# Per-head state products, a state decayed on GpSimd, and other places for a chunk's steps, in linear attention followed by an MLP

## The chip, the cores and the metric

One core of a Trainium2 chip. The metric is device time in microseconds (us) of one execution, the median of several runs. The core has TensorE (PE, matrix products; PEld is its weight load), VectorE (DVE), ScalarE (ACT), GpSimd (POOL) and SyncE (SP). They run side by side, each with its own instruction queue, and are tied together by semaphores. GpSimd and SyncE also issue the DMAs here.

## The reference

```python
# q, k, v: [4, 8, 768, 64] f32, lam: [8]; blocks of 64 positions, per head h
intra = (qb @ kb.T) * Dmask            # Dmask[i, j] = lam**(i - j) for i >= j, else 0
out   = intra @ vb + (qb * lam**(pos + 1)) @ kv_state
kv_state = lam**block * kv_state + (kb * lam**(block - 1 - pos)).T @ vb
# x: the heads' outputs side by side, [3072, 512]
h = x @ w_in                           # w_in [512, 2048]
g = 0.5 * h * (1 + erf(h / sqrt(2)))   # exact GELU
return g @ w_out                       # w_out [2048, 512], result [3072, 512] f32
```

The attention is a recurrence along the sequence: the 64 x 64 state of each head and batch is decayed and added to. The result feeds a two-layer MLP.

## The kernel before

**Chunks and groups.** The kernel works on chunks of C = 128 positions with all 8 heads: 24 chunks, numbered n, 6 per batch (`c.sb` is the place within the batch; the state starts anew at `sb` 0, and `sb` 5 needs no next state). Four chunks (M = 4) make a group of 512 rows for the MLP, so there are 6 groups. Matrix operands are bf16; the loads cast from f32 while they run, and are issued by GpSimd (L65 for q, k and v; L87 and L91 for slices of the two weights).

**A chunk's steps.** `begin` takes the loaded tiles, and `decay_k` makes k_dec (k times a decay) on GpSimd, or on ScalarE for chunks 0 and 1. k^T and q^T are made by TensorE in `transposes` (L178) for chunks 0 to 7, and by DMA in `dma_transposes` (L191 to L193) from chunk 8 on; q_hat is made on GpSimd there. `scores` (L200) multiplies k^T and q^T by pairs of heads into PSUM, and VectorE writes the masked result sc_m (L204). `next_state` forms the state for the next chunk. `outputs` adds, in PSUM, the product of state and q^T and the product of v and sc_m (L262), and the result goes to x_t, the MLP's input (L266 on ScalarE for the first four chunks, L268 on VectorE after).

**The state.** For chunks 0 to 2, `next_state` makes k_dec^T v per head (L215, eight matmuls of 64 columns), one VectorE add gives the new state (L227), and ScalarE makes a decayed copy, old (L230). The state's product in `outputs` is eight matmuls on 64 x 64 quarters of the array (L258). From chunk 4 on, the state is block-diagonal, two heads in each 128 x 128 block: `next_state_full` makes the product in four full matmuls (L237), VectorE adds the former state (tmp, L244) and multiplies by lam_blk, which holds the decay on the diagonal blocks and 0 elsewhere (L245), and `outputs` uses four full matmuls (L252). Chunk 3 crosses over: its state is written into first_blk, of which only the diagonal blocks are filled (L220).

**Order.** The schedule is manual: on each engine the instructions run in the order in which the program emits them. The opening, L341 to L386, is written out by hand: chunks 0 to 3, with idle matmuls (`keep_warm`, L350) between them. In the program, GpSimd's part is: the loads of chunks 0 to 3, w_in slice 0, k_dec of chunks 2 and 3, and then w_in slices 1 to 3, w_out slices 0 to 3 and (L418) the loads of chunks 4 to 7.

After it the MLP runs, group after group, in 32 blocks each: 16 of `mm1` (L280, four matmuls of 512 columns, then GELU on ScalarE, L282) and 16 quarters of `mm2` (L292; L307 in the last group). The attention of the next group's chunks is laid between these blocks: `todo` holds a step's kind (0 begin, 1 transposes, 2 scores and next state, 3 outputs) and its due time as a fraction of a group, and ahead of each block all steps that are due are emitted. The begin step also issues the loads of chunk n + 4 (`prefetch`). In groups from 1 on, the scores of the chunk with place i are due at 0.04 + 0.25 i, its outputs at 0.25 later (0.965 for the last), so the outputs of one chunk and the scores of the next are emitted together.

Of the kernel before, what the change touches and what calls it, by code (L numbers as in the profile page):

```python
# [8 lines left out]
F32 = mybir.dt.float32  # L9
BF16 = mybir.dt.bfloat16  # L10
ALU = mybir.AluOpType
ACT = mybir.ActivationFunctionType
# [3 lines left out]
def kernel(  # L16
# [10 lines left out]
    nc = tc.nc  # L27

    B, H, S, D = q.shape
    d_model, d_ff = moe_w_in.shape  # L30
    C = 128
    NB = S // C
    NCH = B * NB
    HP = H // 2
# [4 lines left out]

    M = 4  # L40
    NG = NCH // M
    assert NG * M == NCH and M < NB

    ctx.enter_context(tc.manual_schedule())

    consts = ctx.enter_context(tc.tile_pool(name="consts", bufs=1))
    w_pool = ctx.enter_context(tc.tile_pool(name="w", bufs=1))
    qkv_pool = ctx.enter_context(tc.tile_pool(name="qkv", bufs=8))
    work_pool = ctx.enter_context(tc.tile_pool(name="work", bufs=3))
# [52 lines left out]
    nc.vector.tensor_scalar(negj, pos, -1.0, None, op0=ALU.mult)  # L102
    nc.vector.tensor_scalar(cmj, pos, -1.0, float(C), op0=ALU.mult, op1=ALU.add)

    lam_blk = consts.tile([128, HP, 128], F32)
    first_blk = consts.tile([128, HP, 128], BF16)
    nc.vector.memset(lam_blk, 0.0)
    nc.vector.memset(first_blk, 0.0)


    ln = consts.tile([128, H], F32)
    ln_col = consts.tile([128, HP], F32)
# [2 lines left out]
    lam_m = consts.tile([128, H], F32)  # L115
    lam_k = consts.tile([128, H], F32)
    lam_c = consts.tile([128, HP], F32)
# [3 lines left out]
    for hi in range(2):  # L121
        p = slice(hi * D, (hi + 1) * D)
# [5 lines left out]
    nc.scalar.activation(lam_c, ln_col, ACT.Exp, scale=float(C))  # L128
    nc.scalar.activation(lam_p, ln, ACT.Exp, scale=pos)
    lam_c_b = lam_c[:, :, None].to_broadcast((128, HP, D))  # L130

    def make_lam_blk():
        for hi in range(2):
            p = slice(hi * D, (hi + 1) * D)
            nc.vector.tensor_copy(lam_blk[p, :, p], lam_c_b[p])

    def make_dmask():
        nc.vector.tensor_mul(dmask, cmask[:, None, :].to_broadcast((128, H, C)),
# [7 lines left out]
    states = {}  # L146

    def bank(shape, dtype, tag, name):
        return ps.tile(shape, dtype, tag=tag, name=name, bufs=2 if tag in ("sc", "mh", "mo") else 1)

    def begin(n, early=False):
        c = Chunk()
        c.n, c.sb, c.early = n, n % NB, early
        c.q, c.k, c.v = (raw.pop((n, name)) for name in "qkv")
        return c

    def decay_k(c, eng):

        if c.sb == NB - 1:
            return  # L160
        c.k_dec = work_pool.tile([128, H, D], BF16, tag="kd", name="k_dec")
        if eng is nc.scalar:
            for h in range(H):
                nc.scalar.activation(c.k_dec[:, h, :], c.k[:, h, :], ACT.Copy, scale=lam_k[:, h:h + 1])
        else:
            scale = lam_k if c.early else lam_m
            eng.tensor_mul(c.k_dec, c.k, scale[:, :, None].to_broadcast((128, H, D)))  # L167

    def transposes(c):
        if c.early:  # L170

            t_ps = [bank([128, HP, C], BF16, tag, "t_ps") for tag in ("mh", "mo")]
        else:
            both = bank([128, 2, HP, C], BF16, "t", "t_ps")
            t_ps = [both[:, 0], both[:, 1]]
        for dst, src in zip(t_ps, (c.k, c.q)):
            for hp in range(HP):
                nc.tensor.transpose(dst[:, hp, :], src[:, 2 * hp:2 * hp + 2, :], ident)  # L178
        c.kT = work_pool.tile([128, HP, C], BF16, tag="kT", name="kT")
        c.qT = work_pool.tile([128, HP, C], BF16, tag="qT", name="qT")  # L180
        if c.early and c.n % 2:
            nc.scalar.copy(c.kT, t_ps[0])
        else:
            nc.vector.tensor_copy(c.kT, t_ps[0])  # L184
        nc.vector.tensor_mul(c.qT, t_ps[1], lam_q)  # L185

    def dma_transposes(c):
        c.kT = work_pool.tile([128, HP, C], BF16, tag="kT", name="kT")
        c.qT = work_pool.tile([128, HP, C], BF16, tag="qT", name="qT")
        q_hat = work_pool.tile([128, H, D], BF16, tag="qh", name="q_hat")  # L190
        nc.sync.dma_start_transpose(out=c.kT, in_=c.k.rearrange("p h d -> p (h d)"))  # L191
        nc.gpsimd.tensor_mul(q_hat, c.q, lam_p[:, :, None].to_broadcast((128, H, D)))  # L192
        nc.sync.dma_start_transpose(out=c.qT, in_=q_hat.rearrange("p h d -> p (h d)"))  # L193
# [12 lines left out]
    def next_state(c):  # L206
        if c.sb == NB - 1:
            return
        if not c.early:
            return next_state_full(c)  # L210
        kv_ps = bank([128, HP, D], F32, "t", "kv_ps")
        for hp in range(HP):
            for hi in range(2):
                h = 2 * hp + hi
                nc.tensor.matmul(kv_ps[hi * D:(hi + 1) * D, hp, :], c.k_dec[:, h, :], c.v[:, h, :],  # L215
                                 start=True, stop=True)
        if c.n == M - 1:
            for hi in range(2):
                p = slice(hi * D, (hi + 1) * D)
                nc.vector.tensor_add(first_blk[p, :, p], kv_ps[p], states[c.n][1][p])  # L220
            states[c.n + 1] = first_blk, None
            return
        new = work_pool.tile([128, HP, D], BF16, tag="state", name="state")
        if c.sb == 0:
            nc.vector.tensor_copy(new, kv_ps)
        else:
            nc.vector.tensor_add(new, kv_ps, states[c.n][1])  # L227
        old = work_pool.tile([128, HP, D], F32, tag="old", name="old")
        for hp in range(HP):
            nc.scalar.activation(old[:, hp, :], new[:, hp, :], ACT.Copy, scale=lam_c[:, hp:hp + 1])  # L230
        states[c.n + 1] = new, old

    def next_state_full(c):

        kv_ps = bank([128, HP, 128], F32, "t", "kv_ps")
        for hp in range(HP):
            nc.tensor.matmul(kv_ps[:, hp, :], c.k_dec[:, 2 * hp:2 * hp + 2, :], c.v[:, 2 * hp:2 * hp + 2, :],  # L237
                             start=True, stop=True)
        new = work_pool.tile([128, HP, 128], BF16, tag="state_f", name="state")
        if c.sb == 0:  # L240
            nc.vector.tensor_mul(new, kv_ps, lam_blk)
        else:
            tmp = work_pool.tile([128, HP, 128], F32, tag="tmp", name="tmp")
            nc.vector.tensor_add(tmp, kv_ps, states[c.n][0])  # L244
            nc.vector.tensor_mul(new, tmp, lam_blk)  # L245
        states[c.n + 1] = new, None

    def outputs(c, x_t, off):
        o_ps = bank([128, HP, C], F32, "o", "o_ps")
        if c.sb > 0 and not c.early:  # L250
            for hp in range(HP):
                nc.tensor.matmul(o_ps[:, hp, :], states[c.n][0][:, hp, :], c.qT[:, hp, :],  # L252
                                 start=(hp == 0), stop=False, skip_group_check=True)
        elif c.sb > 0:
            for hp in range(HP):
                for hi in range(2):
                    p = slice(hi * D, (hi + 1) * D)
                    nc.tensor.matmul(o_ps[p, hp, :], states[c.n][0][p, hp, :], c.qT[p, hp, :],  # L258
                                     start=(hp == 0), stop=False, skip_group_check=True)
        for hp in range(HP):  # L260
            for hi in range(2):
                nc.tensor.matmul(o_ps[hi * D:(hi + 1) * D, hp, :], c.v[:, 2 * hp + hi, :], c.sc_m[:, hp, hi, :],  # L262
                                 start=(c.sb == 0 and hp == 0), stop=True, skip_group_check=True)
        x_o = x_t[:, :, off * C:(off + 1) * C]
        if c.early:
            nc.scalar.copy(x_o, o_ps)  # L266
        else:
            nc.vector.tensor_copy(x_o, o_ps)  # L268
# [73 lines left out]
    live = {}  # L342
# [34 lines left out]
    scores(live[3])  # L377
    keep_warm(5)
    outputs(live[3], xT[0], 3)
    make_lam_blk()  # L380
    next_state(live[3])
    keep_warm(1)
    for s in range(1, NS):
# [5 lines left out]
    total = NK2 * 4 * M * C + M * NK2 * 512  # L389
    todo = []  # L390
    for n in range(M, NCH):
        g, i = n // M - 1, n % M
        if g == 0:
            fs = [0.66 + 0.34 * (i + f) / M for f in (-0.5, 0.0, 0.5, 1.05)]
        else:
            at = 0.04 + 0.25 * i
            fs = [at - (0.15 if n == 2 * M else 0.32), None, at, at + 0.25 if i < M - 1 else 0.965]
        todo += [(round((g + f) * total), -kind, n) for kind, f in enumerate(fs) if f is not None]
    todo.sort()

    def step(minus_kind, n):
        kind = -minus_kind
        g = n // M - 1
        if kind == 0:
            live[n] = begin(n)
            if g > 0:
                dma_transposes(live[n])
            decay_k(live[n], nc.gpsimd)
            prefetch(n + 4)
        elif kind == 1:  # L410
            transposes(live[n])
        elif kind == 2:
            scores(live[n])
            next_state(live[n])
        else:
            outputs(live[n], xT[g + 1], n % M)
# [44 lines left out]
```

## Time and profile before

| | us |
|---|---|
| median of 3 runs | 224.43 |
| lowest, highest | 223.63, 224.9 |
| the profiled execution: time | 223.63 |
| its span, first to last instruction | 221.9 |

| engine | busy us | share of the span |
|---|---|---|
| TensorE | 208.5 | 94% |
| TensorE weight load | 104.1 | 47% |
| GpSimd | 104.8 | 47% |
| ScalarE | 87.7 | 40% |
| VectorE | 77.4 | 35% |

In the profile's lines an instruction group is named by engine, source line and output<-inputs, with the partitions x elements of its tiles. A timeline line gives the start, the time until the group's end, the line and operation, and in brackets the idle time before it with what ended it. A line of waits gives the total, the number and the longest. PEclk is the granted TensorE clock in tenths, in 40 slices of the span; DMA is the mean busy share of the 16 DMA engines in the same slices. Matmuls overlap in the pipeline, so what a group costs TensorE is the time from its start to the start of the next one.

### The profile page before, as it was taken

How to read it: one execution, taken by the hardware profiler on the slowest of the kernel's cores; microseconds unless marked ns; L12 is line 12 of the kernel's file. 1: busy time of each engine (PE TensorE's matmuls, PEld its weight loads, DVE VectorE, ACT ScalarE, POOL GpSimd, SP SyncE). 2: the span in 40 equal slices, each digit the busy share in tenths (PEclk: the TensorE clock that was granted, in tenths of full speed). 3: DMA queues.
4: the chain of work that ended last, by engine and by line, in shares of the span. 5: the costliest groups of instructions: out<-in, count | busy, mean ns of one | idle time of the engine just before them, and what ended most of it. 6: DMA issues, size and time to landing. Idle time of an engine off the chain costs nothing.

```text
span 221.9 us, 3569 instructions
## 1 busy us (share of the span) xinstructions
PE 208.5 (94%) x1423; PEld 104.1 (47%) x1447; DVE 77.4 (35%) x128; ACT 87.7 (40%) x168; POOL 104.8 (47%) x120
## 2 busy tenths in 40 slices
PE   7789999599799999999999999999999999999993
PEld 2355444255445454444455444444545544444452
DVE  5587000458841462233364243035235233100000
ACT  6895763110246611155511355412365321467121
POOL 8998343899999999084981535031100000000000
PEclk9699999969999999999999999999999999999999
DMA  5999999999999999959999997013242012100112
GB/s 38 148 155 191 203 205 179 155 199 151 151 185 164 132 105 170 160 113 152 76 113 144 72 155 105 3 47 96 96 96 47 3 47 78 64 0 3 47 49 95
DMA packets 100272, 24.35 MB, mean 110 GB/s; under 512 B 92960, under 2 KB 97312, under 8 KB 100256
## 3 DMA queue, kind: packets, MB, share of 16 engines
q0 software_dynamic: 79104, 13.64, 84.3%
q1 hardware_dynamic: 21152, 10.50, 21.9%
q8 instruction: 11, 0.18, 0.3%
q14 instruction: 5, 0.04, 0.1%
HBM read 27.27 MB, written 6.29 MB: 151 GB/s over the span
## 4 chain that ended last, share of the span: by engine, by line
PE 89%; DMA 4%; DVE 2%; POOL 2%; issue 1%; ACT 1%; POOLq 0%; DVEq 0%
PE h_ps L280 37%; PE o_ps L292 35%; PE sc_ps L200 4%; PE o_ps L262 3%; PE kv_ps L237 2%; DMA q_t<-in_q_dram 2%; PE idle_ps L350 2%; PE o_ps L252 2%; PE t_ps L178 2%; DMA qT<-q_hat 2%; PE o_ps L307 2%; DVE qT L185 1%; DVE sc_m L204 1%; POOL k_dec L167 1%; ACT x_t L266 0%
## 5 line engine op out<-in xcount | busy, mean ns | idle before, releaser
L280 PE MATMUL h_ps<-x_t,w_in_t 128*128 128x512 bf16 x374 | 84.5, 379 | 2.3 <-DVE x_t L268 1.6
L292 PE MATMUL o_ps<-w_out_t,g_t 128*128 128x512 bf16 x355 | 82.6, 381 | 0.9 <-issue 0.2
L282 ACT ACTIVATE g_t<-h_ps 128x512 bf16<-128x512 f32 x96 | 57.3, 597 | 35.6 <-PE h_ps L280 35.6
L280 PEld LDWEIGHTS <-w_in_t 128*128 128x128 bf16 x384 | 37.1, 98 | 45.3 <-issue 2.0
L292 PEld LDWEIGHTS <-g_t 128*128 128x128 bf16 x368 | 34.9, 98 | 39.9 <-issue 0.6
L297 ACT COPY o_sb<-o_ps 128x512 f32<-128x512 f32 x23 | 13.5, 586 | 88.5 <-PE o_ps L292 85.6
L268 DVE CAST x_t<-o_ps 128x512 bf16<-128x512 f32 x20 | 13.8, 690 | 72.3 <-PE o_ps L262 67.0
L204 DVE TENSOR_TENSOR sc_m<-sc_ps,dmask 128x512 bf16<-128x512 f32 x48 | 30.8, 683 | 13.5 <-PE sc_ps L200 13.2
L65 POOL DMA_DIRECT2D v_t<-in_v_dram x24 | 21.3, 889 | 8.4 <-PE o_ps L262 4.6
L192 POOL TENSOR_TENSOR q_hat<-q_t,lam_p 128x512 bf16<-128x512 bf16 x16 | 16.9, 1054 | 17.4 <-DMA qT<-q_hat 17.3
L167 POOL TENSOR_TENSOR k_dec<-k_t,lam_m 128x512 bf16<-128x512 bf16 x16 | 16.8, 1050 | 16.2 <-PE kv_ps L237 10.3
L65 POOL DMA_DIRECT2D k_t<-in_k_dram x24 | 22.1, 920 | 3.9 <-DMA w_out_t<-in_moe_w_out_dram 2.0
L65 POOL DMA_DIRECT2D q_t<-in_q_dram x24 | 21.5, 896 | 4.6 <-DMA w_out_t<-in_moe_w_out_dram 3.3
L350 PE MATMUL idle_ps<-idle 128*128 128x512 bf16 x26 | 9.9, 507 | 1.2 <-DVE idle L94 1.2
L200 PE MATMUL sc_ps<-qT,kT 64*128 64x128 bf16 x192 | 9.7, 222 | 1.3 <-DVE qT L185 1.3
L245 DVE TENSOR_TENSOR state<-tmp,lam_blk 128x512 bf16<-128x512 f32 x13 | 10.5, 809 | 0.4
L262 PE MATMUL o_ps<-sc_m,v_t 128*64 128x128 bf16 x192 | 10.1, 228 | 0.0
L184 DVE COPY kT<-t_ps 128x512 bf16<-128x512 bf16 x6 | 2.5, 422 | 20.8 <-PE t_ps L178 20.6
L200 PEld LDWEIGHTS <-kT 64*128 64x128 bf16 x192 | 5.7, 95 | 6.8 <-issue 3.0
L237 PE MATMUL kv_ps<-v_t,k_dec 128*128 128x128 bf16 x64 | 6.4, 222 | 2.1 <-POOL k_dec L167 2.1
L244 DVE TENSOR_TENSOR tmp<-kv_ps,state 128x512 f32<-128x512 f32 x12 | 8.2, 681 | 0.0
L262 PEld LDWEIGHTS <-v_t 128*64 128x64 bf16 x192 | 6.2, 111 | 3.1 <-issue 1.0
(56 smaller groups left out, 83.8 us busy)
## 6 DMA issues: line engine op xcount, KB each, us to landing
out_dram<-o_sb SPq DMA_DIRECT2D x23, 256.0 KB, 2.1
k_t<-in_k_dram POOLq DMA_DIRECT2D x24, 128.0 KB, 5.2
q_t<-in_q_dram POOLq DMA_DIRECT2D x24, 128.0 KB, 5.8
v_t<-in_v_dram POOLq DMA_DIRECT2D x24, 128.0 KB, 6.1
w_in_t<-in_moe_w_in_dram POOLq DMA_DIRECT2D x4, 512.0 KB, 8.3
w_out_t<-in_moe_w_out_dram POOLq DMA_DIRECT2D x4, 512.0 KB, 15.2
kT<-k_t SPq DMA_TRANSPOSE x16, 5.0
qT<-q_hat SPq DMA_TRANSPOSE x16, 4.2
```

Of the source, the lines that this page charges most:

```text
L65: nc.gpsimd.dma_start(raw[n, name], chunk_of(name, n))
L167: eng.tensor_mul(c.k_dec, c.k, scale[:, :, None].to_broadcast((128, H, D)))
L192: nc.gpsimd.tensor_mul(q_hat, c.q, lam_p[:, :, None].to_broadcast((128, H, D)))
L200: nc.tensor.matmul(sc_ps[hi][:, hp, :], c.kT[p, hp, :], c.qT[p, hp, :], start=True, stop=True)
L204: nc.vector.tensor_mul(c.sc_m[:, :, hi, :], sc_ps[hi], dmask_r[:, :, hi, :])
L262: nc.tensor.matmul(o_ps[hi * D:(hi + 1) * D, hp, :], c.v[:, 2 * hp + hi, :], c.sc_m[:, hp, hi, :], start=(c.sb == 0 and hp == 0), stop=Tru ...
L268: nc.vector.tensor_copy(x_o, o_ps)
L280: nc.tensor.matmul(h_ps, w_in_t[:, ki, kf * 128:(kf + 1) * 128], x_t[:, ki, :], start=(ki == 0), stop=(ki == NK1 - 1))
L282: nc.scalar.activation(g_t[:, kf, :], h_ps, ACT.Gelu)
L292: nc.tensor.matmul(om[io], g_t[:, kf, io * C:(io + 1) * C], w_out_t[:, kf, :], start=(kf == 0), stop=(kf == NK2 - 1))
L297: nc.scalar.copy(o_sb, om[io])
L350: nc.tensor.matmul(idle_ps, idle[:, :128], idle, start=True, stop=True)
```

## The change

It has been described as a new order of the opening (scores of a chunk ahead of the next chunk's transposes, evacuations of k^T shared by VectorE and ScalarE, idle matmuls up to the first MLP block). The opening's order on TensorE is the same in both kernels; the diff changes the following:

- The block-diagonal state is taken out: lam_blk, first_blk, their two memsets, `make_lam_blk` and `next_state_full`. All chunks use the per-head products (eight matmuls each) for the state and for its use in `outputs`.
- VectorE forms the new state with one add (a copy at `sb` 0). For chunks from 3 on the decayed copy old is made by one GpSimd multiply of 128 x 256 elements, where a later add needs it (`sb` under 4). ScalarE still does it for chunks 0 to 2.
- k_dec uses the factor lam_k for all chunks.
- In groups from 1 on, the due times are spread evenly over 0.97 of the group: scores of chunk place i at 0.2425 (i + 0.35), outputs at 0.2425 (i + 0.75), begin at 0.2425 (i - 1), or 0.2425 (i - 0.45) for chunk 8. In group 0's blocks (chunks 4 to 7) the times are as they were. Steps due at the same time are emitted in the order of their kinds, and no longer in the reverse.

```diff
     def next_state(c):
         if c.sb == NB - 1:
             return
-        if not c.early:
-            return next_state_full(c)
         kv_ps = bank([128, HP, D], F32, "t", "kv_ps")
         ...
-        if c.n == M - 1:
-            for hi in range(2):
-                p = slice(hi * D, (hi + 1) * D)
-                nc.vector.tensor_add(first_blk[p, :, p], kv_ps[p], states[c.n][1][p])
-            states[c.n + 1] = first_blk, None
-            return
         new = work_pool.tile([128, HP, D], BF16, tag="state", name="state")
         ...
         old = work_pool.tile([128, HP, D], F32, tag="old", name="old")
-        for hp in range(HP):
-            nc.scalar.activation(old[:, hp, :], new[:, hp, :], ACT.Copy, scale=lam_c[:, hp:hp + 1])
+        if c.early and c.n < M - 1:
+            for hp in range(HP):
+                nc.scalar.activation(old[:, hp, :], new[:, hp, :], ACT.Copy, scale=lam_c[:, hp:hp + 1])
+        elif c.sb < NB - 2:
+            nc.gpsimd.tensor_mul(old, new, lam_c_b)
         states[c.n + 1] = new, old
     ...
     def outputs(c, x_t, off):
         o_ps = bank([128, HP, C], F32, "o", "o_ps")
-        if c.sb > 0 and not c.early:
-            for hp in range(HP):
-                nc.tensor.matmul(o_ps[:, hp, :], states[c.n][0][:, hp, :], c.qT[:, hp, :],
-                                 start=(hp == 0), stop=False, skip_group_check=True)
-        elif c.sb > 0:
+        if c.sb > 0:
             for hp in range(HP):
                 for hi in range(2):
     ...
     outputs(live[3], xT[0], 3)
-    make_lam_blk()
     next_state(live[3])
     keep_warm(1)
     for s in range(1, NS):
     ...
         g, i = n // M - 1, n % M
-        if g == 0:
-            fs = [0.66 + 0.34 * (i + f) / M for f in (-0.5, 0.0, 0.5, 1.05)]
-        else:
-            at = 0.04 + 0.25 * i
-            fs = [at - (0.15 if n == 2 * M else 0.32), None, at, at + 0.25 if i < M - 1 else 0.965]
-        todo += [(round((g + f) * total), -kind, n) for kind, f in enumerate(fs) if f is not None]
+        first, end = (0.66, 1.0) if g == 0 else (0.0, 0.97)
+        at = lambda f: (g + first + (end - first) * (i + f) / M) * total
+        fs = (-0.5, 0.0, 0.5, 1.05) if g == 0 else (-0.45 if n == 2 * M else -1.0, 0.0, 0.35, 0.75)
+        todo += [(at(f), kind, n) for kind, f in enumerate(fs)]
     todo.sort()
```

More of the change, by code (lines that the diff above doesn't have):

```diff
@@ L41 @@
     NG = NCH // M
-    assert NG * M == NCH and M < NB
+    assert NG * M == NCH
     ctx.enter_context(tc.manual_schedule())
@@ L103 @@
     nc.vector.tensor_scalar(cmj, pos, -1.0, float(C), op0=ALU.mult, op1=ALU.add)
[L105 to L108, printed above, removed]
     ln = consts.tile([128, H], F32)
@@ L130 @@
     lam_c_b = lam_c[:, :, None].to_broadcast((128, HP, D))
-    def make_lam_blk():
-        for hi in range(2):
-            p = slice(hi * D, (hi + 1) * D)
-            nc.vector.tensor_copy(lam_blk[p, :, p], lam_c_b[p])
     def make_dmask():
@@ L165, in decay_k @@
         else:
-            scale = lam_k if c.early else lam_m
-            eng.tensor_mul(c.k_dec, c.k, scale[:, :, None].to_broadcast((128, H, D)))
+            eng.tensor_mul(c.k_dec, c.k, lam_k[:, :, None].to_broadcast((128, H, D)))
     def transposes(c):
@@ L216, in next_state @@
                                  start=True, stop=True)
-        if c.n == M - 1:
-            for hi in range(2):
-                p = slice(hi * D, (hi + 1) * D)
-                nc.vector.tensor_add(first_blk[p, :, p], kv_ps[p], states[c.n][1][p])
-            states[c.n + 1] = first_blk, None
-            return
         new = work_pool.tile([128, HP, D], BF16, tag="state", name="state")
@@ L228, in next_state @@
         old = work_pool.tile([128, HP, D], F32, tag="old", name="old")
-        for hp in range(HP):
-            nc.scalar.activation(old[:, hp, :], new[:, hp, :], ACT.Copy, scale=lam_c[:, hp:hp + 1])
-        states[c.n + 1] = new, old
-    def next_state_full(c):
-        kv_ps = bank([128, HP, 128], F32, "t", "kv_ps")
-        for hp in range(HP):
[L237 to L241, printed above, removed]
-        else:
[L243 to L246, printed above, removed]
+        if c.early and c.n < M - 1:
[3 more added lines that the diff above has]
+            nc.gpsimd.tensor_mul(old, new, lam_c_b)
+        states[c.n + 1] = new, old
     def outputs(c, x_t, off):
         o_ps = bank([128, HP, C], F32, "o", "o_ps")
-        if c.sb > 0 and not c.early:
-            for hp in range(HP):
-                nc.tensor.matmul(o_ps[:, hp, :], states[c.n][0][:, hp, :], c.qT[:, hp, :],
-                                 start=(hp == 0), stop=False, skip_group_check=True)
-        elif c.sb > 0:
+        if c.sb > 0:
             for hp in range(HP):
@@ L392, with step @@
         g, i = n // M - 1, n % M
-        if g == 0:
-            fs = [0.66 + 0.34 * (i + f) / M for f in (-0.5, 0.0, 0.5, 1.05)]
-        else:
-            at = 0.04 + 0.25 * i
-            fs = [at - (0.15 if n == 2 * M else 0.32), None, at, at + 0.25 if i < M - 1 else 0.965]
-        todo += [(round((g + f) * total), -kind, n) for kind, f in enumerate(fs) if f is not None]
+        first, end = (0.66, 1.0) if g == 0 else (0.0, 0.97)
+        at = lambda f: (g + first + (end - first) * (i + f) / M) * total
+        fs = (-0.5, 0.0, 0.5, 1.05) if g == 0 else (-0.45 if n == 2 * M else -1.0, 0.0, 0.35, 0.75)
+        todo += [(at(f), kind, n) for kind, f in enumerate(fs)]
     todo.sort()
-    def step(minus_kind, n):
-        kind = -minus_kind
+    def step(kind, n):
         g = n // M - 1
@@ L410, in step @@
         elif kind == 1:
-            transposes(live[n])
+            if g == 0:
+                transposes(live[n])
         elif kind == 2:
```

## The prediction

> **What bounds the kernel now.** I read the page first (engine shares, then slices, then the chain of waits), after it the waits of TensorE, and last the timelines of TensorE and GpSimd around each wait.
>
> ```profile
> PE 208.5 (94%) x1423; PEld 104.1 (47%) x1447; DVE 77.4 (35%) x128; ACT 87.7 (40%) x168; POOL 104.8 (47%) x120
> ...
> PEclk9699999969999999999999999999999999999999
> DMA  5999999999999999959999997013242012100112
> ```
>
> TensorE is the bound as an average. The DMA row adds that the engines are full from the second slice to about 130 us, so the opening is a race with the loads.
>
> ```profile
> PE kv_ps L237 <- POOL k_dec L167: 2.1, 1, 2.1
> PE h_ps L280 <- DVE x_t L268: 1.6, 1, 1.6
> PE t_ps L178 <- DMA q_t<-in_q_dram: 1.4, 1, 1.4
> PE sc_ps L200 <- DVE qT L185: 1.3, 2, 1.0
> ```
>
> These are nearly all of TensorE's waits, and all end before 62 us. After that TensorE runs without a gap: every instruction added there is time, and no shorter VectorE step saves any. The wait of 2.1 us is the key one. It ends at 44.32, when GpSimd has made k_dec of chunk 4:
>
> ```profile
> 14.36 1.04 POOL L167 TENSOR_TENSOR k_dec<-k_t,lam_k 128x512 bf16<-128x512 bf16 x1 [0.46 <-DMA k_t<-in_k_dram]
> 15.35 2.28 POOL L87 DMA_DIRECT2D w_in_t<-in_moe_w_in_dram  x3
> 17.61 3.00 POOL L91 DMA_DIRECT2D w_out_t<-in_moe_w_out_dram  x4
> 20.57 0.92 POOL L65 DMA_DIRECT2D k_t<-in_k_dram  x1
> 22.60 0.88 POOL L65 DMA_DIRECT2D q_t<-in_q_dram  x1 [1.11 <-DMA w_in_t<-in_moe_w_in_dram]
> ...
> 42.32 0.87 POOL L65 DMA_DIRECT2D v_t<-in_v_dram  x1 [0.41 <-PE sc_ps L200]
> 43.21 1.05 POOL L167 TENSOR_TENSOR k_dec<-k_t,lam_m 128x512 bf16<-128x512 bf16 x1
> ```
>
> GpSimd issues in order: weight slices 1 to 7 leave right behind the k_dec of chunk 3, and the later loads each wait for a landing. By the landing records w_in slice 0 lands at 19.8 and slice 1 at 22.3, each further slice 2.5 us on, then a tile of k, q or v every 0.9 us. This stream has no hole, so k_dec of chunk 4 stands at its end, and TensorE waits for it.
>
> ```profile
> 16.85 0.32 PE L215 MATMUL kv_ps<-v_t,k_dec 128*64 128x64 bf16 x8
> 17.09 0.41 PE L258 MATMUL o_ps<-qT,state 64*64 64x128 bf16 x8
> 17.43 0.41 PE L262 MATMUL o_ps<-sc_m,v_t 128*64 128x128 bf16 x8
> 17.78 0.40 PE L200 MATMUL sc_ps<-qT,kT 64*128 64x128 bf16 x8
> ...
> 92.01 0.39 PE L252 MATMUL o_ps<-qT,state 128*128 128x128 bf16 x4
> 92.33 0.41 PE L262 MATMUL o_ps<-sc_m,v_t 128*64 128x128 bf16 x8
> 92.68 1.04 PE L292 MATMUL o_ps<-w_out_t,g_t 128*128 128x512 bf16 x4
> 93.55 1.89 PE L280 MATMUL h_ps<-x_t,w_in_t 128*128 128x512 bf16 x8
> 95.37 0.40 PE L200 MATMUL sc_ps<-qT,kT 64*128 64x128 bf16 x8
> 95.70 0.40 PE L237 MATMUL kv_ps<-v_t,k_dec 128*128 128x128 bf16 x4
> 95.94 1.24 PE L280 MATMUL h_ps<-x_t,w_in_t 128*128 128x512 bf16 x5
> ```
>
> Start-to-start times are the prices of whole groups: L215 0.24, L258 0.34, L262 0.35, L200 0.33, L252 0.32, L237 0.24. Eight MLP matmuls take 1.82 before L200 (95.37 - 93.55), but 8 x 0.216 = 1.73 otherwise: a change of array shape costs 0.095.
>
> **Part 1: the decayed state moves to GpSimd, ahead of the weight loads.** next_state of chunk 3 now emits a GpSimd multiply (old) and stands in the program before load_w_in(1..3), load_w_out(0..3) and the loads of chunks 4 to 7. GpSimd's queue then waits for the state of chunk 3, and 19 DMA issues stand behind it. The state needs kv (TensorE 20.18 to 20.5) and one VectorE add. Before, two adds began at 20.58; now one of 0.41 ends at about 21.0. The multiply has no row here. Half of k_dec's 1.05 us (half the elements) is 0.53; the dear end is a full 1.05. I take 0.6, near the row of the same form on the same engine. So w_in slice 1 is issued at 21.65 instead of 15.35.
>
> The DMA engines have run dry by then (slice 0 landed at 19.8). The first k tile, also with nothing ahead of it, was issued at 1.39 and served TensorE at 5.09, 3.7 us; a weight slice carries 2.5 - 0.9 = 1.6 us more data, so 5.2 us: landing at 26.85 against 22.32. The stream is late by **S = 4.5 us**. Low end 3.5: the multiply at 0.53, and 0.9 less because the k tile's 3.7 us hold about that much of tail that may not recur. High end 6.2: 0.45 for the dear multiply and 1.27 because slice 0 landed 3.81 after the tile before it, not 2.54.
>
> How much of S reaches the end? First, h_ps block 4 wants slice 1 at 21.03 + 16 x 0.216 = 24.5, so TensorE stalls some 2.3 us there. Then q of chunk 4, landing at 39.8 where TensorE wanted it at 40.2, comes at 44.3. Finally k_dec of chunk 4 comes at 44.27 + S, and TensorE was waiting for it already. All stalls before it are swallowed by this last one, so S counts once and in full: +4.5.
>
> The Trainium skill, "DMA: Bandwidth & Descriptors" (Anatomy of one DMA), gives about 2.0 us plus bytes at 436 GB/s; as an estimate for a slice's 1 MB read that is 4.4 us, not 5.2, and the sum would be 0.8 lower.
>
> **Part 2: narrower state matmuls.** L252 (4 full matmuls) becomes L258 (8 of 64x64), L237 becomes L215. Scores and outputs of neighbouring chunks no longer share a slot in groups from 1 on, so each goes in and out of the MLP's shape by itself. Chunks 8 to 23, from the rows above:
> - Before: 4 lone score slots 0.095 + 0.33 + 0.235 = 0.66, 4 lone output slots 0.317 + 0.347 = 0.66, 12 shared slots. Of these 7 are full, 0.317 + 0.347 + 0.329 + 0.234 = 1.23; 2 lack the state product (1.01) and 3 lack kv (0.99). Sum 18.9.
> - After: 13 score slots with kv 0.095 + 0.329 + 0.245 = 0.67, 3 without 0.425, 14 output slots 0.095 + 0.341 + 0.347 = 0.78, 2 without state 0.44. Sum 21.9.
>
> That is **+3.0**. Chunks 4 to 7: three state products at +0.12 and three kv at +0.01, **+0.4**. All of it is on the path. The rows bound it well: 2.5 to 4.0 with the pairs, the high end being L258's 0.41.
>
> **Part 3: VectorE is relieved.** Per chunk 0.68 + 0.71 (tmp, state) becomes one add of 0.41. Only one place on the path feels it: the end of group 0, where x_t of chunk 7 started at 60.41 behind sc_m (until 59.13), tmp and state, and TensorE waited until 61.14. After: add until 59.55, outputs end at 59.63 with part 2's 0.12, x_t until 60.4. Against a TensorE already 0.12 later this is **-0.8**. The add needs old of chunk 6, which GpSimd does behind the v load that ended at 56.85: done at 57.5, 1.6 us early; both clocks move by S together. If that cover were gone, x_t and group 1 would wait as long as it is late.
>
> **Parts at nothing.** The removed memsets, lam_blk copies and split first_blk add lie on VectorE while TensorE runs idle matmuls or MLP; no later step waits for them, and cover gone they cost at most their 0.75 and 0.4. lam_k for lam_m in k_dec: same form, same 1.05. Moved steps in groups from 1 on: scores 0 to 1 block later (chunk 8: block 3 for 2), outputs 4 blocks earlier for three chunks and 1 for the last; sc_m (1.29) is done within the 3 blocks (2.6 us) between. q_hat of chunk 8 starts 0.6 later behind old; qT landed at 61.5 against 62.96, and scores come 0.86 later, so it stays hidden; uncovered it would cost 0.6. begin(n) moves by at most 0.04 of a group; GpSimd, saturated from 43 to 85 us, sets the times there. Its 13 multiplies add 0.6 to 4.7 us per chunk against TensorE's 8 us, so they hide; SP's transposes and output stores keep more than a block of slack.
>
> **The clock.** Over 41.6 to 45.0 TensorE is busy 1.08 of 3.40 us; in the next 3.4 us the granted clock is 0.50, about 1.7 us lost. Over 58.7 to 62.1, busy 1.79 of 3.40, nothing follows. After the change the stall at 24.5 can bring another such stretch (swallowed by the wait for k_dec), and the old one stays behind k_dec. I take 0, between -1.7 (the stalls split so that no stretch is mostly idle) and +1.7 (a second one behind 49 us).
>
> The Trainium skill, "TensorE: Matmul & The Clock Gate" (Part 1), ties the half clock to an idle window of about 3.4 us; here a gap of 2.06 us, in a window with other idle, sufficed, so the row speaks against counting the new 2.3 us stall as harmless. By the page alone no stretch of half clock would follow, and the sum would be 1.7 lower.
>
> **Sum.** The profiled execution took 223.63 us (span 221.9), 0.8 under the median of 224.43. 223.63 + 4.5 + 3.0 + 0.4 - 0.8 = 230.7. The median lies higher, so I add half of that 0.8: **231.1**.
>
> **Rivals.**
> 1. GpSimd's loads aren't held back (S = 0): 231.1 - 4.5 = 226.6. Against it: in the rows each issue follows the instruction before it, and k_dec of chunk 3 held the slices until 15.35. 8 in 100.
> 2. Late multiplies hold VectorE: where old comes behind a whole load batch (4.7 us), the add and the last x_t of a group wait; 1.0 us of cover stands at block 30, so 3.7 us per boundary, 234.8 for one. For it: GpSimd is full until 85 us. Against: 1.6 us of room for chunk 6. 11 in 100.
> 3. Faster: the shape change costs nothing in the new order, because the 0.095 belongs to those sequences, not to the shape. Then the after sum is 13 x (0.234 + 0.147) + 3 x 0.234 + 14 x (0.246 + 0.252) + 2 x 0.252 = 13.1, not 21.9, and the time 231.1 - 8.8 - 0.4 = 221.9. It beats before once over 7 of those 9 us appear. Against it: L258 took 0.34 at each of its places in the opening. 3 in 100.
> 4. Nothing happens on the path: the load stream had hidden slack and the narrow groups pair better, 224.4. Against: TensorE's waits at 40 and 44 us show no slack. 3 in 100.
>
> **Numbers.** The forecast has 75 in 100, its own range 229.2 (S 3.5, half of the clock's gain) to 234.5 (S 6.2, clock +1.7). The whole range, 227.0 to 235.5, takes in rival 2 and nearly rival 1. A difference under 0.5%, 1.1 us, can't be told from none. Faster is rival 3, 0.03; same rival 4, 0.03; slower the rest, 0.94.
>
> **What would show it.** Right: the w_in issues of slices 1 to 3 start at 21 to 22 us; TensorE waits at 24.5 for w_in_t by 2 us or more; kv_ps of chunk 4 at 48 to 50; x_t's wait under 1 us; each later slot pair 0.2 longer. Wrong: the slices still issued at 15.35, TensorE waits past 63 us for VectorE or GpSimd, or the L258 groups under 0.3.

## The result, and the profile after

The changed kernel takes 231.83 us (median of 4, 230.59 to 232.5) against 224.55 (median of 4) for the kernel before: ratio 1.0325, 95% interval 1.027 to 1.0379, so 7.3 us slower. The forecast was 231.1, range 227.0 to 235.5.

The profiled execution after took 232.5 us (span 230.6), the slowest of its four; the one before, 223.63 (221.9), was the fastest of its four. The two profiles therefore differ by 8.7 us of span, more than the medians. Cut at four points that both timelines show, the difference lies here:

| TensorE, start of | before | after | this stage grew by |
|---|---|---|---|
| first MLP block | 21.03 | 20.34 | -0.7 |
| kv_ps of chunk 4 | 44.32 | 49.23 | 5.6 |
| first MLP block of group 1 | 61.14 | 66.69 | 0.6 |
| first MLP block of group 5 | 190.58 | 199.33 | 3.2 |
| end of the span | 221.9 | 230.6 | 0.0 |

GpSimd's timeline of the changed kernel (start, time to the group's end, line, operation, and in brackets the idle time before it):

```profile
14.87 1.04 POOL L156 TENSOR_TENSOR k_dec<-k_t,lam_k 128x512 bf16<-128x512 bf16 x1 [0.98 <-PE sc_ps L189]
20.38 0.61 POOL L214 TENSOR_TENSOR old<-state,lam_c 128x256 f32<-128x256 bf16 x1 [4.47 <-DVE state L208]
20.94 2.28 POOL L87 DMA_DIRECT2D w_in_t<-in_moe_w_in_dram  x3
23.20 2.99 POOL L91 DMA_DIRECT2D w_out_t<-in_moe_w_out_dram  x4
...
48.12 1.05 POOL L156 TENSOR_TENSOR k_dec<-k_t,lam_k 128x512 bf16<-128x512 bf16 x1
```

The queue stands 4.47 us for the state of chunk 3, and the weight slices leave at 20.94 where they had left at 15.35. The other end of the chain is k_dec of chunk 4, at 48.12 instead of 43.21. TensorE's waits in the same profile (total, times, longest):

```profile
PE kv_ps L202 <- POOL k_dec L156: 2.6, 1, 2.6
PE t_ps L167 <- DMA q_t<-in_q_dram: 2.6, 4, 1.2
PE h_ps L245 <- DMA w_in_t<-in_moe_w_in_dram: 2.5, 1, 2.5
...
PE h_ps L245 <- DVE x_t L233: 0.8, 1, 0.8
```

A new wait for w_in_t of 2.5 us has come, more of the waiting for q_t, and the wait for k_dec is still there in full behind them; the wait for x_t has halved. The clock, in stretches of about 3.4 us (length; busy us of TensorE, weight load, VectorE, ScalarE, GpSimd, with the number of instructions; then the granted clock, the DMA share and GB/s):

```profile
24.30:27.70 3.40, 1.25 (x5) 0.60 (x7) 0.00 (x0) 0.48 (x2) 3.40 (x5) 1.00 1.23 200
27.80:31.10 3.30, 3.30 (x9) 1.10 (x8) 0.00 (x0) 1.49 (x3) 1.03 (x2) 0.50 1.24 205
44.80:48.20 3.40, 1.54 (x16) 0.73 (x14) 2.31 (x4) 0.58 (x1) 2.73 (x5) 1.00 2.43 155
48.30:51.60 3.30, 2.37 (x16) 1.20 (x17) 0.42 (x1) 0.09 (x1) 3.30 (x4) 0.50 2.05 191
51.70:55.00 3.30, 3.08 (x25) 1.74 (x25) 1.71 (x3) 0.40 (x1) 3.30 (x5) 0.50 2.43 156
```

In these rows each stretch with much idle time is followed by one at half clock; in the prediction's row of 58.7 to 62.1, busy 1.79 of 3.40, none followed. Behind kv_ps of chunk 4 there are two, not one. And one pair of slots in group 1, from TensorE's timeline:

```profile
69.37 0.40 PE L189 MATMUL sc_ps<-qT,kT 64*128 64x128 bf16 x8
69.70 0.32 PE L202 MATMUL kv_ps<-v_t,k_dec 128*64 128x64 bf16 x8
69.95 2.76 PE L245 MATMUL h_ps<-x_t,w_in_t 128*128 128x512 bf16 x12
72.64 0.41 PE L223 MATMUL o_ps<-qT,state 64*64 64x128 bf16 x8
72.98 0.41 PE L227 MATMUL o_ps<-sc_m,v_t 128*64 128x128 bf16 x8
73.33 1.04 PE L245 MATMUL h_ps<-x_t,w_in_t 128*128 128x512 bf16 x3
```

Start to start: scores 0.33, kv 0.25, state product 0.34, v product 0.35; the twelve MLP matmuls take 2.69, of which 12 x 0.216 = 2.59 is work and 0.10 the change of shape.

### The profile page after: what moved, and what is told of

It reads as the page before. It is cut to its first block, busy times and chain, and to the rows that moved or that the text cites. A ratio compares the mean times of both kernels' runs of the same rounds, so it can differ in the third digit from the quotient of the medians.

```text
span 230.6 us, 3847 instructions
## 1 busy us (share of the span) xinstructions
PE 212.9 (92%) x1555; PEld 101.9 (44%) x1579; DVE 61.8 (27%) x110; ACT 87.6 (38%) x168; POOL 112.1 (49%) x133
## 4 chain that ended last, share of the span: by engine, by line
PE 77%; DMA 10%; POOL 6%; issue 2%; DVE 2%; ACT 1%; POOLq 0%; DVEq 0%
PE o_ps L257 33%; PE h_ps L245 31%; DMA w_out_t<-in_moe_w_out_dram 8%; PE o_ps L227 3%; PE sc_ps L189 3%; PE o_ps L223 3%; DMA q_t<-in_q_dram 2%; PE kv_ps L202 2%; PE o_ps L272 2%; POOL k_t L65 1%; POOL q_t L65 1%; POOL v_t L65 1%; PE t_ps L167 1%; POOL w_in_t L87 1%; POOL w_out_t L91 1%
## 5 line engine op out<-in xcount | busy, mean ns | idle before, releaser
L245 PE MATMUL h_ps<-x_t,w_in_t 128*128 128x512 bf16 x373 | 87.9, 385 | 4.1 <-DMA w_in_t<-in_moe_w_in_dram 2.5
L257 PE MATMUL o_ps<-w_out_t,g_t 128*128 128x512 bf16 x356 | 83.9, 384 | 1.8 <-issue 1.6
L245 PEld LDWEIGHTS <-w_in_t 128*128 128x128 bf16 x384 | 36.5, 99 | 47.6 <-issue 3.5
L257 PEld LDWEIGHTS <-g_t 128*128 128x128 bf16 x368 | 34.4, 99 | 40.5 <-issue 1.8
L214 POOL TENSOR_TENSOR old<-state,lam_c 128x256 f32<-128x256 bf16 x13 | 8.0, 615 | 55.5 <-DVE state L208 32.0
L156 POOL TENSOR_TENSOR k_dec<-k_t,lam_k 128x512 bf16<-128x512 bf16 x18 | 18.9, 1052 | 1.0 <-PE sc_ps L189 1.0
L315 PE MATMUL idle_ps<-idle 128*128 128x512 bf16 x26 | 8.5, 442 | 1.2 <-DVE idle L94 1.2
L202 PE MATMUL kv_ps<-v_t,k_dec 128*64 128x64 bf16 x160 | 6.4, 203 | 2.6 <-POOL k_dec L156 2.6
L223 PE MATMUL o_ps<-qT,state 64*64 64x128 bf16 x160 | 8.4, 226 | 0.2 <-ACT x_t L231 0.2
L223 PEld LDWEIGHTS <-state 64*64 64x64 bf16 x160 | 5.2, 108 | 7.4 <-issue 6.8
```

What stands on the lines that cost most here:

```text
L156: eng.tensor_mul(c.k_dec, c.k, lam_k[:, :, None].to_broadcast((128, H, D)))
L245: nc.tensor.matmul(h_ps, w_in_t[:, ki, kf * 128:(kf + 1) * 128], x_t[:, ki, :], start=(ki == 0), stop=(ki == NK1 - 1))
L257: nc.tensor.matmul(om[io], g_t[:, kf, io * C:(io + 1) * C], w_out_t[:, kf, :], start=(kf == 0), stop=(kf == NK2 - 1))
```

## Experiments

The theory: GpSimd's queue holds the weight loads back (about 5 us), and narrower products in slots of their own cost a fixed sum of TensorE time from chunk 8 on (about 3 us). The main rival: the loads had slack, and the products and slots cost it all.

**1. old of chunk 3 on ScalarE, in the changed kernel**

```diff
-        if c.early and c.n < M - 1:
+        if c.early:
```

> The changed kernel with one edit: old of chunk 3 is made by ScalarE, as for chunks 0 to 2, so that no GpSimd instruction stands between k_dec of chunk 3 and the weight loads. Theory (the loads are held behind that multiply): the first of the three w_in issues starts near 15.4 us, TensorE's wait for w_in_t is gone, kv_ps of chunk 4 starts near 44 us, and the time falls by 4.9 us (the shift of kv_ps) and by up to 1.2 us more if the clock's second slow window goes with it: 225.7 to 227. What remains over the kernel before is the narrower products, about +3.4, less 0.8. Rival (the narrow products and the new slots cost most of it, the loads had slack): under 1.5 us gained, 230.3 or more. Rival (ScalarE's four extra activations delay the first MLP block): the gain is there, but h_ps starts a microsecond later.

Measured: 227.26 us (226.5 to 228.53), 4.6 under the changed kernel by the medians; by the ratios to the kernel before that ran beside each, 1.0158 (1.0113 to 1.0202) against 1.0325, 3.7 us. The slices leave at 15.49, TensorE's wait for w_in_t is gone, and kv_ps of chunk 4 starts at 45.08, 4.2 us earlier than in the changed kernel. The first h_ps starts at 20.71, no later than the 21.03 of the kernel before. The second slow stretch stayed in this profile (44.1 to 51.0).

```profile
14.51 1.04 POOL L156 TENSOR_TENSOR k_dec<-k_t,lam_k 128x512 bf16<-128x512 bf16 x1 [0.60 <-ACT old L212]
15.49 2.29 POOL L87 DMA_DIRECT2D w_in_t<-in_moe_w_in_dram  x3
```

**2. Only the order in GpSimd's queue, in the changed kernel**

```diff
     outputs(live[3], xT[0], 3)
+    for s in range(1, NS):
+        load_w_in(s)
+    for s in range(NS):
+        load_w_out(s)
     next_state(live[3])
     keep_warm(1)
-    (the same two loops)
```

> The changed kernel with only the place of the seven weight loads in the program moved, ahead of next_state of chunk 3; the GpSimd multiply stays and comes after them. Nothing is left out. Theory (it is the order in GpSimd's queue, not the multiply itself): as with old on ScalarE, 225.7 to 227, within 0.5 us of it. Rival (the multiply itself, 0.6 us on GpSimd, or its use, costs the time): no gain, 231 to 232.

Measured: 226.82 us (225.7 to 227.6), 5.0 under the changed kernel by the medians, 4.4 by the ratios (1.0128, 1.0094 to 1.0163, against 1.0325). kv_ps of chunk 4 starts at 45.60, 3.6 us earlier. GpSimd does the same work in another order:

```profile
15.23 2.29 POOL L87 DMA_DIRECT2D w_in_t<-in_moe_w_in_dram  x3
17.50 3.00 POOL L91 DMA_DIRECT2D w_out_t<-in_moe_w_out_dram  x4
20.82 0.61 POOL L214 TENSOR_TENSOR old<-state,lam_c 128x256 f32<-128x256 bf16 x1 [0.32 <-DVE state L208]
```

The multiply costs nothing in itself that can be told; its place does. The rival of slack in the loads falls here.

**3. The hold alone, in the kernel before**

```diff
             states[c.n + 1] = first_blk, None
+            extra = work_pool.tile([128, HP, D], F32, tag="old", name="old")
+            nc.gpsimd.tensor_mul(extra, first_blk[:, :, :D], lam_c_b)
             return
```

> The kernel before with one instruction added: a GpSimd multiply of 128 x 256 elements that reads first_blk, at the same place in the queue as old of chunk 3 in the changed kernel; its result is not used. Products, slots and due times are those of before. Theory: first_blk is done near 21.4, half a microsecond later than the state in the changed kernel, so the loads leave at 22 us, kv_ps of chunk 4 comes 5 to 6 us later, and the clock adds 0 to 1.7: 229.5 to 232. Rival (the loads had slack, or the shift is taken up later): 224.5 to 226.

Measured: 228.08 us (228.05 to 230.16), ratio 1.0219 (1.0169 to 1.027), 4.1 us slower than 223.95 by the medians and 4.9 by the ratio: below what was expected. Two reasons show. The slices left at 20.35, not 22, because this opening ran ahead (kv_ps of chunk 3 at 18.90, against 20.18 in the kernel before) and because the columns that the multiply reads are written by the first of the two adds.

```profile
19.80 0.61 POOL L223 TENSOR_TENSOR old<-first_blk,lam_c 128x256 f32<-128x256 bf16 x1 [4.29 <-DVE first_blk L220]
20.35 2.29 POOL L87 DMA_DIRECT2D w_in_t<-in_moe_w_in_dram  x3
```

On TensorE's timeline:

```profile
48.65 0.40 PE L239 MATMUL kv_ps<-v_t,k_dec 128*128 128x128 bf16 x4 [2.52 <-POOL k_dec L167]
```

The loads left 5.0 us later, and kv_ps came at 48.65, 4.3 us later than in the kernel before. Here only one slow stretch of clock followed it (50.0 to 53.4), so the total moved by little else.

**4. The due times alone, in the kernel before** (with them the order of ties; products and states as before)

```diff
-            at = 0.04 + 0.25 * i
-            fs = [at - (0.15 if n == 2 * M else 0.32), None, at, at + 0.25 if i < M - 1 else 0.965]
-        todo += [(round((g + f) * total), -kind, n) for kind, f in enumerate(fs) if f is not None]
+        at = lambda f: (g + first + (end - first) * (i + f) / M) * total
+        fs = (-0.5, 0.0, 0.5, 1.05) if g == 0 else (-0.45 if n == 2 * M else -1.0, 0.0, 0.35, 0.75)
+        todo += [(at(f), kind, n) for kind, f in enumerate(fs)]
```

> The kernel before with only the due times of the changed kernel: scores and outputs of neighbouring chunks in slots of their own, block-diagonal states kept. Theory (each change of array shape costs 0.095 us): 13 x 0.66 + 3 x 0.425 + 14 x 0.66 + 2 x 0.44 = 20.0 against 18.9, so +1.1 us: 225.6. Rival (shape changes cost nothing in this order): +-0.3 us, 224.2 to 224.9. Rival (the earlier outputs expose waits for VectorE): +3 us or more.

Measured: 226.33 us (225.3 to 227.13), ratio 1.0108 (1.0073 to 1.0142), 2.4 us slower where 1.1 was expected. From the first MLP block of group 1 (62.85) to that of group 5 (193.57) it took 130.72, 1.28 more than before: the slots cost what the rows say. The rest lies ahead of group 1: kv_ps of chunk 4 started at 45.94, with w_out slice 1 landing 3.6 us after slice 0. Why the stream ran late in this kernel isn't settled.

**5. The products alone** (the second experiment, and in it the diff of the fourth the other way round)

> The changed kernel with the weight loads ahead of next_state of chunk 3 (as in the second experiment) and, besides, the due times of the kernel before: what is left of the change are the per-head products, the single VectorE add and old on GpSimd. Theory: by the rows the slots of chunks 8 to 23 sum to 20.7 us against 18.9, chunks 4 to 7 add 0.4 and x_t at the end of group 0 gives back 0.8: 1.4 us over the kernel before, and 1.2 under the second experiment. From the first MLP block of group 1 to that of group 5 it should take 1.8 us longer than before. Rival (the products cost nothing, pairs of quarters overlap): that stretch as before, within 0.3 us.

Measured: 227.37 us (225.29 to 227.66), ratio 1.0128 (1.008 to 1.0176); not 1.2 under the second experiment but 0.5 over it by the medians, and level with it by the ratios. The expectation missed that the order of ties comes with the due times: in the reverse order, old of chunk 6 stands ahead of chunk 7's k_dec and loads, and waits for its state.

```profile
52.76 0.89 POOL L65 DMA_DIRECT2D v_t<-in_v_dram  x1
56.10 0.61 POOL L214 TENSOR_TENSOR old<-state,lam_c 128x256 f32<-128x256 bf16 x1 [2.45 <-DVE state L206]
56.68 1.03 POOL L156 TENSOR_TENSOR k_dec<-k_t,lam_k 128x512 bf16<-128x512 bf16 x1
...
60.35 1.06 POOL L181 TENSOR_TENSOR q_hat<-q_t,lam_p 128x512 bf16<-128x512 bf16 x1
```

q_hat of chunk 8 came at 60.35 (56.86 before), and its scores waited 1.3 us for qT. From those scores (64.35) to group 5 (194.17) it took 129.82 against 127.62 before, 2.2 more; a second, shorter wait for qT is in that. The products thus cost about 2, near the 1.8 of the rows.

**6 and 7. Idle matmuls across the wait for k_dec of chunk 4** (12 in the changed kernel, 9 in the kernel before)

```diff
             scores(live[n])
+            if n == M:
+                idle_ps = bank([128, 512], F32, "o", "idle_ps")
+                for _ in range(12):
+                    nc.tensor.matmul(idle_ps, idle[:, :128], idle, start=True, stop=True)
             next_state(live[n])
```

> The changed kernel with twelve idle matmuls of 512 columns between the scores and the kv products of chunk 4, where TensorE waits 2.6 us for k_dec. Theory (the clock is halved because the 3.4 us window ahead was mostly idle): no slow window follows kv_ps of chunk 4, and of the 2.9 us lost there in the profiled execution nearly all comes back, less at most 0.3 for idle matmuls that run over: 229 to 230.3. Rival (the clock falls for another reason, such as the stall at 24 us): a slow window stays behind 48 us, and the time is 231.5 to 232.5.

> The kernel before with nine idle matmuls at the same place, ahead of the kv products of chunk 4. Theory: the slow window at 45 to 48 us goes, 1.7 us gained: 222 to 222.8. Rival (the clock does not follow the idle share): 224 to 224.6.

Measured: 231.21 us (230.31 to 231.85) in the changed kernel, not to be told from 231.83; 223.6 (222.91 to 225.2) in the kernel before, ratio 0.9985 (0.9952 to 1.0017). Neither gain came. Yet at this place the clock did as the theory said: no slow stretch follows kv_ps of chunk 4 in either kernel. The stretches in the changed kernel with the bridge:

```profile
45.00:48.40 3.40, 3.15 (x22) 1.41 (x20) 1.83 (x3) 0.58 (x1) 2.83 (x4) 1.00 2.43 155
48.60:52.00 3.40, 3.24 (x41) 2.05 (x42) 2.04 (x4) 0.58 (x1) 3.40 (x4) 1.00 2.06 190
```

and among its waits:

```profile
PE sc_ps L189 <- DMA qT<-q_hat: 1.0, 1, 1.0
```

From kv_ps of chunk 4 to group 1 it took 14.8 us (48.62 to 63.45), not 17.5, and then the scores of chunk 8 waited 1.0 us for qT. The other 1.6 us stand in the profile, but the medians of four runs each show 0.6; why isn't settled.

In the kernel before with its bridge, group 1 began at 60.45 instead of 61.14, after a longer wait for x_t (2.2), and the slow stretch came behind that wait instead:

```profile
57.50:60.90 3.40, 1.20 (x16) 0.76 (x15) 2.87 (x4) 0.59 (x1) 3.40 (x5) 1.00 2.90 149
60.90:64.30 3.40, 3.40 (x18) 1.26 (x17) 0.11 (x1) 1.19 (x2) 3.39 (x4) 0.50 1.91 228
```

On TensorE's timeline:

```profile
60.45 3.16 PE L280 MATMUL h_ps<-x_t,w_in_t 128*128 128x512 bf16 x8 [2.20 <-DVE x_t L268]
```

The first MLP matmuls of group 1 took 3.1 us until the scores of chunk 8, where the kernel before took 1.8, and these scores started at 63.55, no earlier than the 62.96 without the bridge. The bridge had moved the slow stretch and not removed it.

**8. k_dec of chunk 4 earlier in the queue, in the kernel before** (chunk 4's step in `todo` leaves out its `begin` and `decay_k` in return)

```diff
-    prefetch(2 * M - 1)
+    prefetch(M + 1)
+    load(M + 2, "k")
+    load(M + 2, "q")
+    live[M] = begin(M)
+    decay_k(live[M], nc.gpsimd)
+    load(M + 2, "v")
+    next_load[0] += 1
+    prefetch(2 * M - 1)
```

> The kernel before with k_dec of chunk 4 taken forward in GpSimd's queue: it stands behind the q load of chunk 6, ahead of the last four load issues, and not behind them. Theory (kv_ps of chunk 4 waits for GpSimd's queue, not for the data of k): k_dec is made at 39 to 40, kv_ps follows the scores at 42.3 without a wait, 2.0 us are gained and with the idle time the slow window, 1.7 us more: 220.2 to 222. Rival (the next thing late, the loads of chunks 5 to 7 or the transposes, takes the place of the wait): 223 to 224.5.

Measured: 223.71 us (222.08 to 226.36), ratio 0.9967 (0.9929 to 1.0005): no gain that can be told. The profiled execution took 225.7 us, 2.0 over the median, so its later waits need not be those of the others. k_dec is made at 39.27, kv_ps follows the scores at 42.04, no slow stretch follows there, and group 1 begins at 58.64. The longest waits of TensorE are now:

```profile
PE sc_ps L200 <- DMA qT<-q_hat: 2.8, 1, 2.8
PE h_ps L280 <- DVE x_t L268: 2.0, 1, 2.0
```

And on GpSimd:

```profile
56.37 1.06 POOL L192 TENSOR_TENSOR q_hat<-q_t,lam_p 128x512 bf16<-128x512 bf16 x1
```

q_hat of chunk 8 stayed where it was (56.37, before 56.86) behind the loads of chunks 8 to 11, and the scores of chunk 8 stood at 63.31. GpSimd's queue is not the whole of that wait: the DMA that makes qT landed 5.7 us after its issue (57.45 to 63.18), against 3.6 in the kernel before (57.95 to 61.53). Why it took longer isn't settled. The half clock came back behind this wait:

```profile
61.10:64.40 3.30, 1.08 (x15) 0.77 (x16) 0.67 (x2) 0.06 (x1) 3.29 (x4) 1.00 1.62 240
64.50:67.80 3.30, 3.30 (x9) 1.22 (x8) 1.81 (x3) 1.19 (x2) 3.29 (x4) 0.50 1.97 170
```

The rival of this experiment was right in that the next thing late took the place of the wait. That the queue decides it is tested by the ninth.

**9. The queue reordered further, in the kernel before** (as the eighth, and the loads of chunks 10 and 11 behind q_hat and k_dec of chunk 8)

```diff
-            prefetch(n + 4)
+            if n not in (M + 2, M + 3):
+                prefetch(n + 4)
```

> The kernel before with GpSimd's queue reordered: k_dec of chunk 4 taken forward as in the eighth experiment, and the loads of chunks 10 and 11 put behind q_hat and k_dec of chunk 8. Theory (with the wait for k_dec gone, the next thing late was qT of chunk 8, behind the same queue): q_hat of chunk 8 is made near 51 to 53 instead of 56 to 57, its qT lands before 58, the scores of chunk 8 wait for nothing, and the stream of MLP blocks in group 1 starts at 58.6 as there but keeps it: 221 to 222.5. Rival (GpSimd's load issues are simply too many and the next q_hat, of chunk 9, is late by as much): 223.5 to 224.5.

Measured: **221.15 us** (220.62 to 223.09), ratio 0.9864 (0.9816 to 0.9913): 1.4% under the kernel before, and clear of the eighth (0.9929 to 1.0005). TensorE's waits:

```profile
PE h_ps L280 <- DVE x_t L268: 1.5, 1, 1.5
...
PE sc_ps L200 <- DMA qT<-q_hat: 1.1, 1, 1.1
```

GpSimd's timeline:

```profile
50.81 1.04 POOL L192 TENSOR_TENSOR q_hat<-q_t,lam_p 128x512 bf16<-128x512 bf16 x1 [0.56 <-DMA q_t<-in_q_dram]
...
60.67 1.12 POOL L192 TENSOR_TENSOR q_hat<-q_t,lam_p 128x512 bf16<-128x512 bf16 x1
```

q_hat of chunk 8 is made at 50.81 and its scores run at 59.14 without a wait; what is left is a wait of 1.1 us for the qT of chunk 9, whose q_hat came at 60.67 behind nine load issues. From the opening's end on no slow stretch is in this profile (granted clock 1.00 from 11 to 215 us), so part of the gain is the 1.7 us that the half clock cost the kernel before. The edit moved k_dec and q_hat; q_hat alone was not tried.

**10. x_t of chunk 7 on ScalarE as well**

```diff
-        if c.early:
+        if c.early or c.n == 2 * M - 1:
             nc.scalar.copy(x_o, o_ps)
```

> As the ninth, and x_t of chunk 7 is written by ScalarE instead of VectorE. Theory (the wait of 1.6 to 2 us at the end of group 0 is VectorE's queue, sc_m and the two state steps of chunk 7): the wait falls to 0.7, and the time by 0.9 to 1.3 us against the ninth: 220 to 221.5. Rival (qT or the loads take it back): no gain.

Measured: 222.49 us (220.2 to 224.04), ratio 0.9878 (0.982 to 0.9935), no gain over the ninth. The wait for x_t fell to 0.7 as expected, and the scores of chunk 9 waited 2.6 us for qT instead of 1.1, with half clock behind that wait (69.0 to 72.4). The rival held in this profile, which took 223.29 us; two of the six runs took 220.2 and 220.3.

**11. The same opening in the changed kernel** (the diffs of experiments 2, 8, 9 and 10 together)

> The changed kernel with the weight loads ahead of next_state of chunk 3, the same reordered queue and x_t of chunk 7 on ScalarE. Theory: the opening costs as in the tenth, and the narrower products and separate slots still cost their 3.0 us from chunk 8 on and 0.4 before: 3.2 to 3.6 us over the tenth, 223.5 to 225. Rival (what the rows charge to shapes was in truth the opening's waits): within 1 us of the tenth.

Measured: 226.02 us (224.78 to 230.4), 3.5 over the tenth by the medians, inside what was expected, and 5.1 by the ratios (1.0104 against 0.9878), over it; both medians lie about 1 us above their ranges. From group 1 to group 5 it took 134.24 us, of which 1.5 is a wait for the qT of chunk 9; the other 132.7 are the changed kernel's, against 129.44. With the waits of the opening shortened, the products and slots keep 3.3 us, as by the rows.

**12. The kernel before, once more**

> The kernel before, profiled a second time, to see how far the load stream and the waits of one execution repeat. Theory: kv_ps of chunk 4 starts within 1 us of 44.3, at the landing of the stream of weights; a difference in the total of up to 1 us has its place there. Rival (the opening repeats exactly, and the times differ later): kv_ps within 0.1 us.

Measured: 224.07 us (223.66 to 225.71), ratio 1.0003 (0.9964 to 1.0042). In this profile kv_ps of chunk 4 starts at 44.50 (44.32 in the first), and from group 1 to group 5 it takes 61.36 to 190.80, 129.44 again, to the hundredth. The stages of the table agree within 0.2 us in these two profiles. Between executions they can differ more: the 23 runs of this kernel beside it took 222.0 to 226.0 us.

## Why the prediction was right, point by point

**The load stream (4.5).** Shown: experiments 1 and 2 took 3.7 to 5.0 us off the changed kernel by taking one instruction out of the loads' way, and experiment 3 put 4.1 to 4.9 on the kernel before by adding one. kv_ps of chunk 4 moved by 3.6 to 4.3 us in these three. Of its terms, the multiply took 0.61 (0.6 was said) and left the queue at 20.94 (21.65), because this opening ran 0.7 ahead of the other profile's (in all fourteen profiles the first MLP block starts between 19.7 and 21.1, in either kernel). Issue to landing of slice 1 was 5.44 (5.2), landing 26.38 (26.85), so S was 4.1 there. It grew to 4.9 at k_dec of chunk 4, because w_out slice 1 landed 3.4 us after slice 0 and not 2.5. That late slice is no part of the change: seven of the fourteen profiles have it, the first of the kernel before has not. So the size was right within half a microsecond, and in part by luck: an earlier landing and a late slice nearly cancel. The shorter estimate from the Trainium skill's "DMA: Bandwidth & Descriptors" (Anatomy of one DMA), 4.4 us to the landing, was a microsecond short of the measured 5.44.

**That S counts once.** The waits for w_in_t and q_t came and the wait for k_dec kept its size (2.1 before, 2.6 after), as the sum had it. What the prediction didn't see is how near the next limit was: q_hat of chunk 8 on the same queue. Its qT had 1.4 us to spare in the kernel before (landed at 61.53, scores at 62.96) and 2.8 in the changed one (66.58 and 69.37). Experiments 6 and 8 brought group 1 forward by 2.6 and 2.5 us and ended in waits for qT of 1.0 and 2.8; experiment 7 brought it forward by 0.7 and lost that to the half clock behind the wait for x_t. For the forecast it did no harm, since queue and TensorE moved late together; the gain came only when q_hat was moved as well (experiment 9).

**Products and slots (3.4).** 3.20 from group 1 to group 5 against 3.0, the same 132.64 in the profiles of the changed kernel and of experiments 1 and 2. Alone, the slots cost 1.28 and the products about 2. Rival 3, that shapes cost nothing in the new order, is out: the row of the changed kernel has 0.10 for the change of shape, and from group 1 to group 5 the time grew and did not fall.

**x_t (-0.8).** The wait fell from 1.6 to 0.8. Right, with old of chunk 6 made in time behind the loads; experiment 5 shows what the other order of ties does.

**The clock (0, between -1.7 and +1.7).** In the profiled execution two slow stretches follow kv_ps of chunk 4, 5.85 us at half clock against 3.4, so about +1.2. The first, at 27.8, was swallowed as said. Not every execution has the second: the mean granted clock of the four ran from 0.978 to 0.993, and the median lies 0.7 under the profiled time. The row was the better guide than the page of the Trainium skill, "TensorE: Matmul & The Clock Gate" (Part 1): waits of 2.5 and 2.6 us were each followed by half clock. That the forecast needed no clock term is in part luck. Between the two profiles the terms as measured, 4.9, 3.2, -0.8 and 1.2, with the 0.4 of chunks 4 to 7, make 8.9 us, and 8.9 was measured (223.63 to 232.5); the medians are 7.3 us apart, near the 7.1 without the clock.

**Rivals 1, 2 and 4** did not come: the loads were held, after the first block of group 1 no wait of TensorE is for old or VectorE, and the time moved far out of the 0.5%.

## What to carry to other kernels

An instruction that waits, put into the queue that also issues DMAs, costs not its own 0.6 us but the distance to what it waits for, for every load behind it: look at what follows it in the queue, not at what it does. A queue order is a schedule: the same work on GpSimd gave 231.8 and 226.8 us. When a wait is taken away, ask which instruction stands next in that same queue; here moving k_dec alone gained nothing that can be told, and moving q_hat with it did (221.15). Ask too where the idle time goes: in experiments 7, 8 and 10 it gathered at the next wait, and the half clock came behind that one.

## What was not expected of the hardware

After a mostly idle stretch the half clock lasted 3.4 us when the stretch that followed was filled (3.39 of 3.40 us busy, kernel before) and 6.8 us when it began with idle time (2.37 of 3.30, kernel after; 2.47 of 3.41 in experiment 1). How much idle time it takes doesn't come out of the busy share alone: in experiment 4 a stretch busy 1.58 of 3.40 us (39.2 to 42.6) brought no half clock, and in the opening of experiment 2 one busy 2.21 of 3.40 (11.0 to 14.4) did.

A slice of weights that lands every 2.5 us was now and then 3.3 to 3.7 us behind its forerunner (w_out slice 1 in the changed kernel and in experiments 1 to 4, 6 and 8). The packet records show one 16 KB fetch of instructions, about 0.9 us long, in that part of the stream in each profile, also in those where no slice was late. That it delays a slice when it falls on the engine that is last already would fit, but was not tested.
